# Transposing k by DMA instead of on TensorE, from the seventh step on, in a fused retention and MLP kernel

## The chip, the cores and the metric

The kernel runs on one core of one Trainium2 chip. The metric is the device time of one execution in microseconds (us), lower is better. Most executions of a kernel agree within about 1%; those that came out over 1.5% above the fastest of their kernel are marked slow and named below. A version is called faster or slower when the ratio of its times to those of the kernel before is clear of 2%.

The engines are called as in the profile: PE (TensorE matmuls), PEld (its weight loads), DVE (VectorE), ACT (ScalarE), POOL (GpSimd), SP (SyncE). SP computes nothing; it issues DMAs, one after the other, and waits where an issue needs somebody else's result.

## The reference

```python
# attention part: B = 8, H = 8 heads, S = 576, D = 64, all float32
scores = q @ k.transpose(0, 1, 3, 2) / sqrt(D)
ret    = scores * Dmat                    # Dmat = gamma_h ** (i - j) for i >= j, else 0
x      = (ret @ v)                        # -> (4608 tokens, 512)
# MLP part
h    = x @ w_in                           # 512 -> 1024
solu = h * softmax(h)
ln   = (solu - mean) / sqrt(var + 1e-6) * g_ln
out  = ln @ w_out                         # 1024 -> 512
```

## The kernel before

The work is cut into 36 steps of the attention part (`i`: 256 tokens, four heads) and 36 tiles of 128 tokens of the MLP part (`t`). Every small piece of work is an operation with a name: `ldk5` loads k of step 5, `sk5` scales it to float16 on POOL, `T5` transposes q and k of step 5 on PE, `qe5` copies the result from PSUM to SBUF on ACT, `S5` makes the scores, `M1_5` and `M2_5` are the two GEMMs of tile 5, `out5` stores it. Each engine works through a fixed list of these names. The first half of each list (`FIRST`) is written out, the rest follows from sort keys. A small list model with a duration for each kind of operation (`DUR`) only decides the program order; the chip decides the time.

```python
DUR = dict(T=0.45, ..., qe=1.0, ..., ld=0.89, ldw=1.34, out=0.72, lm=0.42)
CAP = dict(raw=5, qk16=3, v16=4, tp=1, qkT=3, s=1, ...)        # buffers of each kind

def load(i, nm, src):                       # 128 x 512 float32, issued by SP
    ...
    if wi < 2:
        nc.sync.dma_start(out=t, in_=...)                       # one issue, 256 KB
    else:
        for r in range(4):                                      # four issues of 64 KB
            nc.sync.dma_start(out=t[32 * r : 32 * r + 32], in_=...)

def qk_tp(i):                               # T: eight 128x128 transposes on PE
    tp = pools["tp"].tile([P, 2, 2, 2, P], F16, ...)
    for n, src in enumerate((d["q16"], d["k16"])):
        for hp in range(2):
            for j in range(2):
                nc.tensor.transpose(out=tp[:, n, hp, j],
                                    in_=src[:, j, 2 * hp : 2 * hp + 2, :], identity=ident)

def qk_ev(i):                               # qe: 1024 columns, PSUM to SBUF, on ACT
    nc.scalar.copy(out=d["qkT"], in_=d["tp"])

def x_ev(i):                                # xe: attention output, input of the first GEMM
    nc.scalar.copy(out=d["xT"].rearrange("p c h q -> p c (h q)"), in_=d["av"][:, :, 0:256])

def store(t):                               # out: even and odd rows apart, two issues a tile
    for j in range(2):
        q_dma = nc.scalar if t == NT - 1 and j else nc.sync
        if wi < 2:
            q_dma.dma_start(out=out[r0 : r0 + P, :].rearrange("(q j) m -> j q m", j=2)[j],
                            in_=tk[t]["osb"][64 * j : 64 * j + 64])
        ...                                 # wi == 2: two pieces each, four issues a tile

op(f"T{i}",  "PE",  "T",  [f"sq{i}", f"sk{i}"], ...)
op(f"qe{i}", "ACT", "qe", [f"T{i}"], ...)
op(f"S{i}",  "PE",  "S",  [f"qe{i}"], ...)
```

The softmax here doesn't subtract the row's maximum and nothing guards it: scores larger than these inputs give would overflow.

Of the kernel before, what the change touches and what calls it, by code (L numbers as in the profile page):

```python
# [10 lines left out]
F16 = mybir.dt.float16  # L11
P = 128
# [1 line left out]

DUR = dict(
    T=0.45, L=0.45, M1=1.73, M2=1.73, I=0.23, S=0.23, V=0.23, K=0.14, G=0.1,
    qe=1.0, xe=0.59, ex=1.22, le=1.0, oe=0.69, wi=0.6, wg=0.66, cva=0.6,
    mask=1.22, st_a=0.29, so=1.22, bn=1.68, od=0.7, wib=0.55, wgd=0.5, WM=1.73, nw=0.62, wf=0.66, wp=1.04, sqd=0.7, gc=0.2,
    sq=1.03, sk=1.03, st_b=0.4, cast=0.84, rs=0.6, cv=0.61,
    ld=0.89, ldw=1.34, out=0.72, lm=0.42,  # L20
)
PE_OUT = 0.2
PER = 5.36
START = dict(SP=2.3)
WARM = 31.0
NE = 14

FIRST = dict(
    ACT=(
        "cv0 qe0 cv1 qe1 xe0 wi1a wi2a wi0a xe1 wi3a ex0 qe2 wg0 le0 wg2 qe3 wg4 wg6 ex1 xe2 "  # L30
        "nw1 nw0 xe3 qe4 wf1 ex2 qe5 wf3 le1 xe4 qe6 wf2 ex3 le2 xe5 oe0 qe7 wf0 ex4 le3 xe6 "
        "qe8 ex5 le4 xe7 qe9 oe1 ex6 le5 oe2 qe10 xe8 ex7 le6 xe9 qe11 oe3 ex8 le7 oe4 wf6 "
        "qe12 xe10 wf4 ex9 le8 xe11 oe5 wf7 qe13 ex10 le9 xe12 wf5 qe14 oe6 ex11 le10 xe13 "
        "oe7 qe15 oe8 ex12 le11 xe14 qe16 oe9 ex13 le12 xe15 qe17 oe10 ex14 le13"
    ),
    DVE=(
        "gc sq0 sa0 sd0 sq1 mask0 wi1b sa1 sd1 mask1 wi2b wi0b wi3b sa2 sd2 so0 mask2 wg1 sa3 "
        "sd3 wg3 wg5 wg7 mask3 so1 bn0 sa4 sd4 bn1 mask4 so2 od0 sa5 sd5 mask5 bn2 sa6 sd6 "
        "so3 mask6 od1 bn3 sa7 sd7 so4 mask7 od2 bn4 sa8 sd8 so5 mask8 bn5 sa9 sd9 so6 od3 "
        "mask9 bn6 so7 od4 sa10 sd10 mask10 bn7 so8 od5 sa11 sd11 mask11 bn8 sa12 so9 sd12 "  # L40
        "od6 mask12 bn9 sa13 sd13 so10 od7 mask13 bn10 so11 sa14 sd14 od8 bn11 mask14 so12 "
        "sa15 sd15 od9 mask15 bn12 so13 od10 mask16 bn13 so14"
    ),
    PE=(
        "G K0 T0 S0 T1 I0 V0 K1 S1 I1 V1 M1_0 T2 K2 S2 L0 I2 V2 K3 T3 M1_1 S3 WM I3 V3 K4 T4 "
        "M1_2 S4 T5 M2_0 L1 I4 V4 K5 S5 T6 M1_3 I5 V5 K6 S6 L2 M2_1 T7 M1_4 I6 V6 K7 S7 L3 "
        "M2_2 T8 M1_5 I7 V7 K8 S8 L4 M2_3 T9 M1_6 I8 V8 K9 L5 S9 T10 M1_7 L6 I9 M2_4 V9 K10 "
        "S10 T11 M1_8 L7 I10 M2_5 V10 K11 S11 T12 M1_9 L8 I11 V11 K12 S12 M2_6 T13 M1_10 I12 "
        "V12 K13 S13 L9 M2_7 T14 M1_11 I13 L10 M2_8 V13 K14 S14 T15 M1_12 L11 M2_9 I14 V14 "
        "K15 S15 T16 M1_13 L12 I15 S16 V15 M2_10 T17 M1_14 L13 I16 S17 V16 M2_11"  # L50
    ),
    POOL=(
        "sk0 sk1 sm0 sc0 sm1 sc1 sq2 sk2 cv2 sk3 sm2 sc2 cv3 sq3 sm3 sc3 sk4 sq4 cv4 sq5 sk5 "
        "sm4 sc4 sq6 rs0 cv5 sk6 sq7 sm5 sc5 cv6 cv7 sk7 sm6 sk9 sc6 sk8 sq8 wp0 rs1 sm7 sc7 "
        "cv8 sq9 cv10 cv9 wp3 sm8 sk10 sc8 cv12 wp2 sq10 sq11 sq12 sm9 sc9 sk11 cv11 sk12 wp1 "
        "sm10 sc10 sk13 rs2 sq13 sq14 cv14 sm11 sc11 sk14 rs3 wp6 sm12 sc12 cv13 sq16 cv15 "
        "cv16 sm13 sc13 wp4 sk15 sq15 sk16 wp5 rs4 sm14 sc14 sq17 wp7 sk17 rs5 cv17 sm15 sc15 "
        "sq18 sk18 cv18 sq19 sk19 cv19"
    ),
    SP=(  # L60
        "ldk0 ldv0 ldq0 ldk1 ldq1 lm ldv1 lwi1 lwi2 lwi0 lwi3 ldq2 ldk2 ldv2 ldk3 lwo0 ldv3 "
        "ldq3 lwo2 lwo4 lwo6 ldk4 ldq4 ldv4 ldq5 ldk5 ldq6 ldv5 ldk6 ldv7 ldq7 ldq9 ldk7 ldk8 "
        "ldv6 ldq10 ldv8 ldk9 ldq11 ldq8 ldv10 ldk10 ldv11 ldq14 ldk11 ldk14 ldv9 ldv12 ldq12 "
        "ldk12 ldk13 ldq16 out0 out1 ldk17 ldv16 ldq15 ldq13 ldv13 out2 ldv14 ldq17 ldk16 "
        "out4 ldv15 ldk15 out3 out5 out7 out6 ldv17 ldv18 ldq19 ldk18 ldv19 ldq18 ldk19 ldq20 "
        "out8 ldk20 ldv20 out9 ldq21 ldk21 ldv21"
    ),
)
HOP = 0.06
# [104 lines left out]
def kernel(  # L174
# [10 lines left out]
    nc = tc.nc  # L185
    B, H, S, D = q.shape
    NTOK, DM = out.shape
    DFF = moe_w_in.shape[1]
    ACT = mybir.ActivationFunctionType
# [2 lines left out]
    small_np, masks_np, id_np = _np_tables()  # L192


    CAP = dict(raw=5, qk16=3, v16=4, tp=1, qkT=3, s=1, ret=2, xy=1, gw=6, s160=4, s161=9, tt=2,
               xT=5, h=1, e=2, oc=2, solu=3, sml=8, lnT=4, o=1, osb=3)
    pools = {}
    PS = bass.MemoryType.PSUM
# [36 lines left out]
    st = [dict() for _ in range(NS)]  # L235
    tk = [dict() for _ in range(NT)]
# [43 lines left out]
    def cast_v(i, copy):  # L280
        t = pools["v16"].tile([P, 4, 2, D], F16, tag="v16", name="v16")
        copy(out=t, in_=st[i]["vr"])
        st[i]["v16"] = t

    def qk_tp(i):
        d = st[i]
        tp = pools["tp"].tile([P, 2, 2, 2, P], F16, tag="tp", name="tqk")
        for n, src in enumerate((d["q16"], d["k16"])):
            for hp in range(2):
                for j in range(2):  # L290
                    nc.tensor.transpose(  # L291
                        out=tp[:, n, hp, j], in_=src[:, j, 2 * hp : 2 * hp + 2, :], identity=ident
                    )
        d["tp"] = tp

    def qk_ev(i):
        d = st[i]
        d["qkT"] = pools["qkT"].tile([P, 2, 2, 2, P], F16, tag="qkT", name="qkT")
        nc.scalar.copy(out=d["qkT"], in_=d["tp"])  # L299


    ee = [slice(0, 64), slice(64, 128)]
# [34 lines left out]
    def scores(i):  # L337
        d = st[i]
        s_ps = pools["s"].tile([P, 2, 2, 2, P], FP, tag="s", name="s_ps")
        sv = s_ps.rearrange("p e h j (a q) -> p e h j a q", a=2)  # L340
        qkT = d["qkT"]
        for hp in range(2):
            for j in range(2):
                for c in range(2):
                    for e in range(2):
                        nc.tensor.matmul(  # L346
                            out=sv[ee[c], e, hp, j], lhsT=qkT[ee[e], 1, hp, j, ee[c]],
                            rhs=qkT[ee[e], 0, hp, :, ee[c]], start=True, stop=True,
                        )
        d["s"] = s_ps  # L350
# [142 lines left out]
    def mm2(t):  # L493
# [6 lines left out]
        for c in range(8):  # L500
            nc.tensor.matmul(  # L501
                out=d["o"], lhsT=d["lnT"][:, c], rhs=(w2g16 if t < NE else w2c16)[:, c], start=(c == 0), stop=(c == 7)
            )
# [10 lines left out]
    def o_ev(t):  # L514
        d = tk[t]
        d["osb"] = pools["osb"].tile([P, DM], FP, tag="osb", name="o_sb")
        nc.scalar.activation(  # L517
            out=d["osb"], in_=d["oc"] if t < NE else d["o"], func=ACT.Copy,
            scale=ws[t // 2]["rs"][:, t % 2 : t % 2 + 1],
# [59 lines left out]
    def op(name, eng, kind, deps, key, emit, bufs=()):  # L579
        key = rank.get(name, PER * key[0] + key[1])  # L580
        ops.append(Op(name, eng, DUR[kind], [x for x in deps if x], key, emit, bufs))

    for i in range(NS):
        w, hf = divmod(i, 2)
        b, wi = wins[w]
        full = wi < 2
# [4 lines left out]
        op(f"sq{i}", "DVE" if early else "POOL", "sqd" if early else "sq", [f"ldq{i}"], (i - 2, 1.8),  # L591
           lambda i=i, e=nc.vector if early else nc.gpsimd: scale(i, "q", 0, e), [("q16", [f"T{i}"])])
        op(f"sk{i}", "POOL", "sk", [f"ldk{i}"], (i - 2, 2.9), lambda i=i: scale(i, "k", 32, nc.gpsimd),
           [("k16", [f"T{i}", f"K{i}" if full else ""])])
        op(f"cv{i}", "ACT" if early else "POOL", "cva" if early else "cv", [f"ldv{i}"], (i - 1, 0.0),
           lambda i=i, c=nc.scalar.copy if early else nc.gpsimd.tensor_copy: cast_v(i, c),
           [("v16", [f"V{i}", f"K{i}" if full else ""])])
        op(f"T{i}", "PE", "T", [f"sq{i}", f"sk{i}"], (i - 1, 2.73), lambda i=i: qk_tp(i), [("tp", [f"qe{i}"])])
        op(f"qe{i}", "ACT", "qe", [f"T{i}"], (i - 1, 3.6), lambda i=i: qk_ev(i), [("qkT", [f"V{i}"])])
        op(f"S{i}", "PE", "S", [f"qe{i}"], (i, 0.3), lambda i=i: scores(i), [("s", [f"mask{i}"])])  # L600
        op(f"mask{i}", "DVE", "mask", [f"S{i}", "lm"], (i, 3.2), lambda i=i: mask(i), [("ret", [f"V{i}"])])
        if full:
            op(f"K{i}", "PE", "K", [f"sk{i}", f"cv{i}"] + [f"V{i - 1}" if i else ""], (i, 0.8), lambda i=i: kv_mm(i))
# [15 lines left out]
    for t in range(NT):  # L619
        w, c = divmod(t, 2)  # L620
# [6 lines left out]
        if c:  # L627
            op(f"rs{w}", "POOL", "rs", [f"bn{t - 1}", f"bn{t}"], (m + 2, 0.77), lambda w=w: rstd(w), [("sml", [f"oe{t}"])])
        op(f"L{t}", "PE", "L", [f"so{t}"], (m + 1, 4.9), lambda t=t: ln_tp(t), [("tp", [f"le{t}"])])
        op(f"le{t}", "ACT", "le", [f"L{t}"], (m + 2, 0.97), lambda t=t: ln_ev(t), [("lnT", [f"M2_{t}"])])  # L630
        o_end = f"od{t}" if t < NE else f"oe{t}"
        op(f"M2_{t}", "PE", "M2", [f"le{t}"] + [f"{'wg' if t < NE else 'wp'}{x}" for x in range(8)], (m + 4, 1.0),
           lambda t=t: mm2(t), [("s" if late(t) else "o", [o_end])])
        if t < NE:
            op(o_end, "DVE", "od", [f"M2_{t}", "nw0"], (m + 4, 2.9), lambda t=t: o_mean(t), [("oc", [f"oe{t}"])])
# [4 lines left out]
    for c in range(4):  # L640
# [4 lines left out]
        out=masks, in_=nc.inline_tensor(masks_np, name="masks").ap().rearrange("p (m j) -> p m j", m=2)))  # L645
    op("G", "PE", "G", ["ldk0"], (0, 0.0), g_tp, [("h", ["gc"])])
    op("gc", "DVE", "gc", ["G"], (0, 1.0), lambda: nc.vector.tensor_copy(out=gln, in_=cur["g_ps"][:, 0:8]))
    for c in range(0, 8, 2):
        op(f"lwo{c}", "SP", "ldw", [], (-2 + c / 8, 0.6), lambda c=c: nc.sync.dma_start(out=w2_f[:, c : c + 2], in_=w2_v[:, c : c + 2]))
        for x in (c, c + 1):  # L650
            op(f"wf{x}", "ACT", "wf", ["gc", "nw1"], (8 + x * 0.75, 1.9), lambda x=x: nc.scalar.activation(
                out=w2_f[:, x], in_=w2_f[:, x], func=ACT.Copy, scale=gln[:, x : x + 1]))
# [5 lines left out]
    for x in range(2):  # L658
        op(f"nw{x}", "ACT", "nw", ["WM"], (5, 1.1), lambda x=x: nc.scalar.activation(
            out=nws[:, x], in_=cur["w_sum"], func=ACT.Copy, scale=1.0 if x == 0 else 1.0 / DFF))  # L660
# [7 lines left out]
    with tc.manual_schedule():  # L668
# [14 lines left out]
        for o in sorted(ops, key=lambda o: start[o.name]):  # L683
            if o.eng == "PE":
                fill = fill and o.name[:2] != "M2"
                if fill and 6.0 < start[o.name] < WARM:
                    for _ in range(int((start[o.name] - end_pe - 0.3) / 0.36)):
# [33 lines left out]
```

## Time and profile before

| | before |
|---|---|
| median, first three runs | 226.03 us (225.61 to 1063.31; the 1063 is one outlier that stays unexplained) |
| PE busy, whole run | 207.0 us of 224.9 (92%) |
| PE busy from 105 to 207 us | 101.86 us of 102 |
| SP in issue entries, 40 to 180 us | 94 of 140 us (67%) |
| POOL waiting for loads, whole run | 13.0 us |

Lines of the page of the kernel before. First busy time and instructions by engine, then busy tenths in 40 slices of the run (with the clock that PE was granted and the mean share of the 16 DMA engines), the main DMA queue with the share of the engines' time that its packets took, the chain of work that ended last, and one group of instructions (busy us, mean ns of one | idle before it):

```profile
span 224.9 us, 7378 instructions
PE 207.0 (92%) x2985; PEld 121.8 (54%) x2985; DVE 181.5 (81%) x320; ACT 163.2 (73%) x238; POOL 151.8 (67%) x231
...
PE   7776989899699999699999999999999999999991
...
PEclk9999999999999999999999999999999999999998
DMA  6999999995576610799988776777763552222324
...
q1 hardware_dynamic: 65200, 41.96, 66.9%
...
PE 63%; DVE 17%; DMA 9%; POOL 4%; issue 2%; SPq 2%; ACT 1%; DVEq 0%; POOLq 0%; ACTq 0%
...
L299 ACT COPY qkT<-tqk 128x1024 f16<-128x1024 f16 x36 | 36.3, 1008 | 9.3 <-PE tqk L291 9.1
```

The second half of the run is PE alone. The chain of waits shows one step of it (start, us, what): second GEMM, transposes of q and k, first GEMM.

```profile
146.42 1.83 PE o_ps L501 x8
148.25 0.45 PE tqk L291 x8
148.70 1.73 PE h_ps L431 x8
```

The windows view of the same kernel (stretch, its length, then busy us of PE, PEld, DVE, ACT, POOL, the clock, the DMA share, GB/s):

```profile
60.00:80.00 20.00, 19.12 (x314) 11.43 (x314) 18.87 (x32) 16.47 (x25) 18.55 (x29) 1.00 0.66 182
...
105.00:207.00 102.00, 101.86 (x1529) 62.26 (x1528) 86.65 (x153) 77.66 (x114) 68.67 (x108) 1.00 0.62 167
```

The timeline of SP's queue (start, us, what). The page has a load of 256 KB landing (all its data in place) 4.6 to 4.8 us after its issue:

```profile
107.29 0.51 SPq L259 DMA_DIRECT2D kr<-in_k_dram  x1
107.89 0.50 SPq L259 DMA_DIRECT2D vr<-in_v_dram  x1
108.48 1.12 SPq L529 DMA_DIRECT2D out_dram<-o_sb  x2
```

The sums are taken record by record from the trace; the timeline merges neighbours of one kind and shows the gaps between them as part of the entry. Some entries are much longer than others of their kind (a load can take over 2 us); they count in full.

### The profile page before, as it was taken

To read this page: it belongs to the slowest core of one execution; us is meant where nothing else is said; L and a number is where in the kernel's file an instruction comes from. 1 tells how busy PE (TensorE), PEld (TensorE's weight loads), DVE (VectorE), ACT (ScalarE), POOL (GpSimd) and SP (SyncE) were. 2 spreads that over 40 slices of the span, in tenths; PEclk is the share of its full clock that TensorE was granted. 3 is DMA by queue.
4 is the path that set the end of the run, shared out by engine and by line. 5 is a ranking of instruction groups with operands and counts; after the bars stand their busy time and mean duration, and the time that the engine had idled before them with its cause. 6 is when DMAs were issued, how large, how long until landed. Compare 5 with 4: busy or idle time off the path is not lost.

```text
span 224.9 us, 7378 instructions
## 1 busy us (share of the span) xinstructions
PE 207.0 (92%) x2985; PEld 121.8 (54%) x2985; DVE 181.5 (81%) x320; ACT 163.2 (73%) x238; POOL 151.8 (67%) x231
## 2 busy tenths in 40 slices
PE   7776989899699999699999999999999999999991
PEld 2433445556455556465666666665666666555440
DVE  6654788999999998999999888888887888876540
ACT  3555889776869988578787777777777777776751
POOL 3429599899989989829578869695968677311010
PEclk9999999999999999999999999999999999999998
DMA  6999999995576610799988776777763552222324
GB/s 176 360 344 348 320 262 287 286 279 157 128 224 173 195 24 13 188 305 293 267 235 247 215 195 192 214 191 191 218 184 109 153 131 52 50 47 60 84 69 119
DMA packets 65635, 42.64 MB, mean 190 GB/s; under 512 B 4024, under 2 KB 59456, under 8 KB 65600
## 3 DMA queue, kind: packets, MB, share of 16 engines
q1 hardware_dynamic: 65200, 41.96, 66.9%
q8 instruction: 23, 0.38, 0.8%
q10 hardware_dynamic: 400, 0.21, 0.5%
q14 instruction: 12, 0.10, 0.2%
HBM read 32.71 MB, written 9.44 MB: 187 GB/s over the span
## 4 chain that ended last, share of the span: by engine, by line
PE 63%; DVE 17%; DMA 9%; POOL 4%; issue 2%; SPq 2%; ACT 1%; DVEq 0%; POOLq 0%; ACTq 0%
PE h_ps L431 21%; PE o_ps L501 21%; PE xy L311 6%; PE tln L480 5%; PE tqk L291 4%; DMA qr<-in_q_dram 4%; DVE solu L451 4%; PE s_ps L346 4%; DVE bs L457 3%; DVE ret L379 3%; DMA vr<-in_v_dram 3%; DMA kr<-in_k_dram 2%; DVE oc L509 2%; SPq L259 2%; DVE w L465 1%
## 5 line engine op out<-in xcount | busy, mean ns | idle before, releaser
L431 PE MATMUL h_ps<-w_in_122,xT 128*128 128x512 f16 x288 | 68.0, 379 | 2.0 <-DVE solu L451 1.9
L451 DVE TENSOR_TENSOR solu<-h_ps,e_sb 128x1024 f16<-128x1024 f32 x36 | 43.9, 1219 | 13.4 <-ACT e_sb L444 13.2
L444 ACT ACTIVATE e_sb<-h_ps 128x1024 f32<-128x1024 f32 x36 | 36.8, 1022 | 18.2 <-PE h_ps L431 17.9
L457 DVE BATCH_NORM_STATS2 bs<-solu 128x6 f32<-128x512 f16 x72 | 46.0, 680 | 0.1
L379 DVE TENSOR_TENSOR ret<-s_ps,masks 128x1024 f16<-128x1024 f32 x36 | 43.7, 1215 | 0.6 <-PE s_ps L346 0.4
L299 ACT COPY qkT<-tqk 128x1024 f16<-128x1024 f16 x36 | 36.3, 1008 | 9.3 <-PE tqk L291 9.1
L431 PEld LDWEIGHTS <-xT 128*128 128x128 f16 x288 | 27.0, 98 | 29.1 <-issue 2.8
L501 PEld LDWEIGHTS <-lnT 128*128 128x128 f16 x288 | 25.9, 98 | 27.2
L488 ACT COPY lnT<-tln 128x1024 f16<-128x1024 f16 x36 | 36.2, 1005 | 3.5 <-PE tln L480 3.5
L501 PE MATMUL o_ps<-w2c_124,lnT 128*128 128x512 f16 x160 | 38.0, 380 | 0.0
L501 PE MATMUL o_ps<-w2g_123,lnT 128*128 128x512 f16 x112 | 26.5, 380 | 0.0
L419 ACT CAST xT<-xy 128x512 f16<-128x512 f32 x36 | 21.4, 594 | 6.6 <-PE xy L311 6.2
L404 POOL TENSOR_TENSOR g<-tt,small 128x128 f32<-128x128 f32 x32 | 13.4, 418 | 15.3 <-DVE tt L400 15.3
L480 PEld LDWEIGHTS <-solu 128*128 128x128 f16 x288 | 18.5, 98 | 8.7 <-DVE solu L451 1.7
L517 ACT ACTIVATE o_sb<-o_ps,rs 128x512 f32<-128x512 f32 x20 | 13.7, 687 | 12.7 <-PE o_ps L501 6.9
L480 PE MATMUL tln<-ident,solu 128*128 128x128 f16 x288 | 22.0, 219 | 0.9 <-DVE solu L451 0.9
L346 PE MATMUL s_ps<-qkT 64*64 64x128 f16 x576 | 14.9, 220 | 0.8 <-ACT qkT L299 0.7
L346 PEld LDWEIGHTS <-qkT 64*64 64x64 f16 x576 | 9.5, 107 | 4.6 <-ACT qkT L299 1.8
L395 DVE TENSOR_TENSOR g<-xy,g 128x128 f32<-128x128 f32 x16 | 4.6, 289 | 8.7 <-PE xy L311 5.2
L400 DVE TENSOR_TENSOR tt<-xy,g 128x128 f32<-128x128 f32 x32 | 9.3, 292 | 2.7 <-ACT xT L419 0.7
L509 DVE SCALAR_TENSOR_TENSOR oc<-nws,mv,o_ps 128x512 f32<-128x512 f32 x14 | 10.3, 738 | 0.2 <-PE o_ps L501 0.2
L517 ACT ACTIVATE o_sb<-oc,rs 128x512 f32<-128x512 f32 x14 | 10.2, 728 | 0.3 <-DMA qr<-in_q_dram 0.3
(507 smaller groups left out, 336.9 us busy)
## 6 DMA issues: line engine op xcount, KB each, us to landing
kr<-in_k_dram SPq DMA_DIRECT2D x32, 256.0 KB, 4.6
vr<-in_v_dram SPq DMA_DIRECT2D x32, 256.0 KB, 4.8
qr<-in_q_dram SPq DMA_DIRECT2D x32, 256.0 KB, 4.8
out_dram<-o_sb SPq DMA_DIRECT2D x64, 128.0 KB, 2.4
w_in_f<-in_moe_w_in_dram SPq DMA_DIRECT2D x4, 512.0 KB, 5.9
w_f<-in_moe_w_out_dram SPq DMA_DIRECT2D x4, 512.0 KB, 8.0
qr<-in_q_dram SPq DMA_DIRECT2D x16, 64.0 KB, 2.3
kr<-in_k_dram SPq DMA_DIRECT2D x16, 64.0 KB, 2.0
```

What stands on the lines that cost most here:

```text
L299: nc.scalar.copy(out=d["qkT"], in_=d["tp"])
L346: nc.tensor.matmul(out=sv[ee[c], e, hp, j], lhsT=qkT[ee[e], 1, hp, j, ee[c]], rhs=qkT[ee[e], 0, hp, :, ee[c]], start=True, stop=True,)
L379: nc.vector.tensor_tensor(out=d["ret"].rearrange("p e h j q -> p (e h) (j q)"), in0=d["s"].rearrange("p e h j q -> p (e h) (j q)"), in1=ma ...
L419: nc.scalar.copy(out=d["xT"].rearrange("p c h q -> p c (h q)"), in_=d["av"][:, :, 0:256])
L431: nc.tensor.matmul(out=h_ps[:, hh], lhsT=st[2 * w + dc // 2]["xT"][:, c, dc % 2], rhs=w_in16[:, dc, hh], start=(dc == 0), stop=(dc == 3),)
L444: nc.scalar.activation(out=d["e"], in_=d["h"], func=ACT.Exp, accum_out=ws[w]["se"][:, c : c + 1])
L451: nc.vector.tensor_tensor(out=d["solu"], in0=d["h"], in1=d["e"], op=ALU.mult)
L457: nc.vector.bn_stats(out=bs[:, half], in_=tk[t]["solu"][:, half * 512 : half * 512 + 512])
L480: nc.tensor.transpose(out=tp[:, c], in_=d["solu"][:, c * P : (c + 1) * P], identity=ident)
L488: nc.scalar.copy(out=d["lnT"], in_=d["tp"])
L501: nc.tensor.matmul(out=d["o"], lhsT=d["lnT"][:, c], rhs=(w2g16 if t < NE else w2c16)[:, c], start=(c == 0), stop=(c == 7))
L517: nc.scalar.activation(out=d["osb"], in_=d["oc"] if t < NE else d["o"], func=ACT.Copy, scale=ws[t // 2]["rs"][:, t % 2 : t % 2 + 1],)
```

## The change

The intent: PE is full, and four of its eight transposes in each step are those of k. From the seventh step on a transposing DMA makes them, from SBUF to SBUF (called "the crossbar" below). PE then has 0.22 us less to do in each of 30 steps, and ACT copies 512 columns instead of 1024. Loads get a sixth buffer, and the lists of all engines are written out for the whole run, ordered with the model for the new program. The diff is shortened: `...` stands for what is cut, and a few one-line changes that follow from those shown are left out.

```diff
-PER = 5.36
+PER = 5.14
+ND = 6
 DUR = dict(
-    qe=1.0, ...
+    T2=0.23, qe=1.0, qe2=0.59, tk=1.05, ...
 FIRST = dict(...)      # all five lists are new, to the end of the run (cut here)
-    CAP = dict(raw=5, qk16=3, v16=4, tp=1, qkT=3, ...
+    CAP = dict(raw=6, qk16=3, v16=4, tp=1, qkT=3, kT=3, ...
+    def k_tp(i):
+        d["kT"] = pools["kT"].tile([P, 2, 2, P], F16, tag="kT", name="kT")
+        nc.sync.dma_start_transpose(
+            out=d["kT"].rearrange("p j h t -> p (j h) t"),
+            in_=d["k16"].rearrange("p j h d -> p (j h d)"),
+        )
-        for n, src in enumerate((d["q16"], d["k16"])):
+        for n, src in enumerate((d["q16"], d["k16"]) if i < ND else (d["q16"],)):
-        nc.scalar.copy(out=d["qkT"], in_=d["tp"])
+        nc.scalar.copy(out=d["qkT"][:, :n], in_=d["tp"][:, :n])
+        dma_k = i >= ND
+        if dma_k:
+            op(f"tk{i}", "SP", "tk", [f"sk{i}"], ..., lambda i=i: k_tp(i), [("kT", [f"S{i}"])])
-        op(f"T{i}", "PE", "T", [f"sq{i}", f"sk{i}"], ...)
+        op(f"T{i}", "PE", "T2" if dma_k else "T", [f"sq{i}"] + ([] if dma_k else [f"sk{i}"]), ...)
-        op(f"S{i}", "PE", "S", [f"qe{i}"], ...)
+        op(f"S{i}", "PE", "S", [f"qe{i}"] + ([f"tk{i}"] if dma_k else []), ...)
```

## The prediction

> **What bounds it now.** Three stretches. (1) Until about 40 us the kernel fills: the windows view gives the DMA engines a share of 0.99 and 1.04 in the first two 20 us stretches, and the chain of waits runs over loads and POOL. (2) From 40 to 104 us DVE is busy 19.2, 18.9 and 18.4 us of each 20 and PE 18.2, 19.1 and 18.0; the chain alternates between DVE and PE, and ten steps (q/k transposes at 48.85 to 105.26 us) take 5.64 us each. (3) From 105 to 207 us PE is busy 100% and the chain is PE alone, about 5.3 us a step: two GEMMs of 1.73 to 1.83, transposes of the normalised tile 0.45, q/k transposes 0.45, scores and state work about 0.9.
>
> **What the change does.** In 30 of 36 steps the four k transposes leave PE. In the timeline the k group starts 0.22 to 0.24 us after the q group, so they cost PE 0.22 us a step, 6.7 us in all. The ACT copy of the transposed q/k (1.01 us for 1024 columns) halves; a 512-column copy (xT, groups view) took 0.59, so ACT loses about 0.4 us a step, 12 us in all, off the chain in stretch 3. DVE and POOL do the same work. SP gets 30 transposing DMAs of 128 KB, SBUF to SBUF, each waiting for POOL's scaled k; scores now wait for that DMA as well. A sixth load buffer lets loads start earlier. The instruction order beyond step 17 is now a fixed list.
>
> **On the critical path.** Stretch 3: the chain holds 17 q/k groups from 111 to 196 us, so 17 x 0.22 = 3.7 us. Stretch 2: DVE work per step is unchanged, so the 0.22 us there is mostly hidden; but at 5.64 us a step there are stalls (POOL waits 4.0 us for a late q load at 101 us; DMA moves only 24 and 13 GB/s about 79 to 90 us), which the new order, the sixth buffer and lighter ACT can partly recover: 1 to 3 us. Tail: nothing. Expected gain about 5.5 us.
>
> **The risk is the DMA.** No trace here has a transposing DMA. The Trainium skill, "VectorE: DVE Perf Modes" (The three transpose paths), gives 1309 ns for one 128x128 block through the crossbar; "Advanced Engine Details and Errata" (X-Bar Transpose) says such DMAs are about as fast as ordinary ones. Ordinary 256 KB loads took 4.6 to 4.8 us to land, so I estimate 2 to 5 us here, queued behind loads. K is scaled well over 5 us before its scores (for example 101.2 to 103.2 scaled, scores of that step after 108), barely enough. If the transposes take several times that of engine time, the loads behind them, at a DMA share of 0.74 to 0.93 in 100 to 140 us, come late and stretch 3 gets holes. SP works in order, so a transpose waiting for POOL also holds back loads.
>
> **Predicted: 220.5 us** (80%: 216 to 228). Faster by over 2%: 0.55; within 2%: 0.30; slower by over 2%: 0.15.
>
> **What would show it.** Right: q transposes alone take 0.22 us; the copy to qkT about 0.59 us; PE still 99 to 100% busy after 105 us with about 5.05 us a step; PE busy total near 200 us; scores hardly wait for the kT DMA; ACT busy near 151 us. Stretch 2 down to about 5.4 us a step.
> Wrong: scores waiting for kT on the chain; DMA share at 1 after 100 us and POOL waiting for loads; SP's wait list headed by POOL's k; kT landing later than 5 us; PE below 97% in stretch 3; or DVE taking over as the bound there (it had 16.2 to 17.2 of 20 us).

## The result, and the profile after

The changed kernel takes 240.1 us (median; 238.98 to 240.56 in four runs) against 226.23 us: a ratio of 1.0615 with a 95% interval of 1.0564 to 1.0667. It is slower by 6%. Ratios here and below are the mean time of one kernel's fast runs over that of the other's of the same rounds, so not quite the ratio of the medians that are quoted.

The lines of the page of the changed kernel that answer to those above. PE is as busy in microseconds, but holes have come into the second half, the clock dips after them, and the chain that was PE for 63% now runs over DMA, POOL and SP's queue:

```profile
span 238.4 us, 7123 instructions
PE 206.8 (87%) x2862; PEld 116.8 (49%) x2862; DVE 177.6 (75%) x320; ACT 151.4 (64%) x238; POOL 151.7 (64%) x231
...
PE   7876899997949986999999798999872799999992
...
PEclk9999999999997999799999999999999599999999
DMA  7999997999589688799997897696877254323073
...
q1 hardware_dynamic: 81520, 45.89, 79.3%
...
PE 39%; DMA 20%; POOL 15%; SPq 14%; ACT 4%; issue 4%; DVE 3%; POOLq 0%; ACTq 0%; DVEq 0%
```

What was to be saved was saved. The groups view, shapes apart, has the copy at 583 ns where it had 1008, and PE's trace has 123 matmuls fewer (30 x 4 = 120 were taken out; a few records can be missing):

```profile
L344 ACT COPY qkT<-tqk 128x512 f16<-128x512 f16 x30 | 17.5, 583 | 9.0 <-PE tqk L335 9.0
```

The windows view shows where it went: PE lost 10.7 of the 102 us of its full stretch.

```profile
60.00:80.00 20.00, 16.90 (x238) 9.66 (x237) 13.65 (x25) 12.97 (x22) 13.41 (x20) 0.91 0.80 192
...
105.00:207.00 102.00, 91.31 (x1345) 53.05 (x1344) 79.57 (x140) 65.00 (x105) 72.34 (x111) 0.97 0.82 184
```

PE's list of waits (us in total, times, longest) is headed by scores that waited for a transposed k:

```profile
PE s_ps L392 <- DMA kT<-k_3927: 5.6, 1, 5.6
PE s_ps L392 <- DMA kT<-k_1415: 3.1, 1, 3.1
...
PE s_ps L392 <- DMA kT<-k_1110: 1.2, 1, 1.2
```

The longest of them can be followed. POOL's timeline has this k scaled by 175.5 us:

```profile
174.46 1.04 POOL L310 TENSOR_TENSOR k_3927<-kr,small 128x512 f16<-128x512 f32 x1
```

SP's timeline shows why its transpose began only at 182.7. It stood in the list behind another step's transpose, the stores of two tiles, a four-part load and one more load, over 7 us of issuing without a pause:

```profile
175.40 2.12 SPq L324 DMA_TRANSPOSE kT<-k_3864  x1
177.62 2.45 SPq L575 DMA_DIRECT2D out_dram<-o_sb  x4
180.12 2.02 SPq L302 DMA_DIRECT2D kr<-in_k_dram  x4
182.19 0.43 SPq L295 DMA_DIRECT2D vr<-in_v_dram  x1
182.72 1.23 SPq L324 DMA_TRANSPOSE kT<-k_3927  x1
```

PE's timeline has the hole of 5.65 us before the scores, and then a second GEMM that lasts 3.59 us in this view where the chain of the kernel before has 1.83; the windows view shows the granted clock at half speed for these four microseconds:

```profile
186.05 0.64 PE L392 MATMUL s_ps<-qkT,kT 64*64 64x128 f16 x16 [5.65 <-DMA kT<-k_3927]
...
187.45 3.59 PE L547 MATMUL o_ps<-w2c_127,lnT 128*128 128x512 f16 x8
```

The windows view over the same microseconds, in two stretches of four:

```profile
182.00:186.00 4.00, 0.00 (x0) 0.00 (x0) 1.23 (x1) 0.83 (x2) 0.56 (x2) 0.76 0.58 144
186.00:190.00 4.00, 3.95 (x30) 2.12 (x31) 3.19 (x6) 1.50 (x2) 3.75 (x7) 0.50 0.16 33
```

The Trainium skill, page "TensorE: Matmul & The Clock Gate" (Why this matters for your kernels), warns of idle gaps of more than about 3 us between matmuls, after which PE falls back to half its clock. This trace agrees in kind: a 5.65 us gap, then 0.50. As a limit the 3 us are not sharp here: the same trace grants half the clock for 3.4 us after a gap of 2.54 us (PE idle from 93.1, half clock from 95.3) and the full clock after one of 2.31 us (from 172.1), and in run e10 below a gap of 3.19 us (from 130.0) passed without a drop. So a late input can cost PE more than its own wait.

SP's issue entries now fill 124 of the 140 us from 40 to 180 (94 before), and POOL waits 25 us for loads (13 before). Over the whole run the 30 transposes hold SP for 39.9 us; all its other entries take 143.9 us, where they took 144.4 before. So the transposes came on top, and nothing made room for them.

### The profile page after: what moved, and what is told of

It reads as the page before. It is cut to its first block, busy times and chain, and to the rows that moved or that the text cites. A ratio compares the mean times of both kernels' runs of the same rounds, so it can differ in the third digit from the quotient of the medians.

```text
span 238.4 us, 7123 instructions
## 1 busy us (share of the span) xinstructions
PE 206.8 (87%) x2862; PEld 116.8 (49%) x2862; DVE 177.6 (75%) x320; ACT 151.4 (64%) x238; POOL 151.7 (64%) x231
## 3 DMA queue, kind: packets, MB, share of 16 engines
q1 hardware_dynamic: 81520, 45.89, 79.3%
## 4 chain that ended last, share of the span: by engine, by line
PE 39%; DMA 20%; POOL 15%; SPq 14%; ACT 4%; issue 4%; DVE 3%; POOLq 0%; ACTq 0%; DVEq 0%
PE o_ps L547 14%; PE h_ps L477 10%; DMA kr<-in_k_dram 6%; DMA qr<-in_q_dram 6%; SPq L295 5%; SPq L302 5%; PE xy L356 4%; PE tln L526 4%; SPq L575 3%; DMA out_dram<-o_sb 3%; PE s_ps L392 2%; POOL w2c_127 L618 2%; PE tqk L335 2%; DMA masks<-masks 2%; DVE solu L497 2%
## 5 line engine op out<-in xcount | busy, mean ns | idle before, releaser
L534 ACT COPY lnT<-tln 128x1024 f16<-128x1024 f16 x36 | 36.5, 1013 | 16.0 <-PE tln L526 15.8
L547 PEld LDWEIGHTS <-lnT 128*128 128x128 f16 x288 | 27.1, 100 | 28.8 <-issue 3.7
L547 PE MATMUL o_ps<-w2c_127,lnT 128*128 128x512 f16 x160 | 39.5, 392 | 0.0
L344 ACT COPY qkT<-tqk 128x512 f16<-128x512 f16 (+1 forms) x36 | 23.6, 654 | 13.7 <-PE tqk L335 13.7
L547 PE MATMUL o_ps<-w2g_126,lnT 128*128 128x512 f16 x112 | 28.4, 399 | 0.0
L526 PE MATMUL tln<-ident,solu 128*128 128x128 f16 x288 | 23.0, 225 | 1.1 <-ACT qkT L344 0.7
L392 PE MATMUL s_ps<-qkT,kT 64*64 64x128 f16 x480 | 12.5, 224 | 10.0 <-DMA kT<-k_3927 5.6
L439 DVE COPY g<-xy 128x128 f32<-128x128 f32 x16 | 4.5, 281 | 12.9 <-PE xy L356 11.0
L392 PEld LDWEIGHTS <-kT 64*64 64x64 f16 x480 | 8.4, 111 | 11.3 <-DMA kT<-k_3927 5.8
```

The source lines that it names most:

```text
L344: nc.scalar.copy(out=d["qkT"][:, :n], in_=d["tp"][:, :n])
L392: nc.tensor.matmul(out=sv[ee[c], e, hp, j], lhsT=kT[ee[e], hp, j, ee[c]], rhs=qkT[ee[e], 0, hp, :, ee[c]], start=True, stop=True,)
L526: nc.tensor.transpose(out=tp[:, c], in_=d["solu"][:, c * P : (c + 1) * P], identity=ident)
L534: nc.scalar.copy(out=d["lnT"], in_=d["tp"])
L547: nc.tensor.matmul(out=d["o"], lhsT=d["lnT"][:, c], rhs=(w2g16 if t < NE else w2c16)[:, c], start=(c == 0), stop=(c == 7))
```

## The experiments

Four theories were to be told apart.

- **S**: SP's single in-order queue is short of issue time. Each transpose takes it 1.2 us, all 30 of them 39.9 us.
- **D**: the crossbar transposes take time on the 16 DMA engines, and the loads behind them come late.
- **L/W**: the dependencies. The scores wait for a landing that takes microseconds (L), or SP stands waiting for POOL's scaled k and holds back loads (W).
- **O**: the new order or the sixth buffer is bad by itself.

The columns of this table: the median; the ratio to the kernel before of the same rounds, with its interval; SP's issue entries from 40 to 180 us; the time that the packets of the SP and ACT queues took on the 16 DMA engines (their shares added, times the span); and POOL's waits for loads. The last three come from the one profiled execution.

| run | median us | ratio (95%) | SP us of 140 | DMA engines us | POOL waits us |
|---|---|---|---|---|---|
| before | 226.2 | 1 | 94 | 152 | 13 |
| changed | 240.1 | 1.062 (1.056 to 1.067) | 124 | 190 | 25 |
| e1 new order, k on PE | 224.9 | 0.991 (0.985 to 0.996) | 94 | 155 | 9 |
| e2 old order, crossbar | 244.2 | 1.075 (1.070 to 1.079) | 116 | 191 | 18 |
| e3 half of the stores from ACT | 234.9 | 1.032 (1.028 to 1.037) | 109 | 186 | 14 |
| e4 plain copy for the crossbar | 233.2 | 1.026 (1.020 to 1.032) | 116 | 169 | 21 |
| e5 crossbar issued from ACT | 235.4 | 1.040 (1.033 to 1.047) | 93 | 197 | 12 |
| e6 = e1 + unused crossbar | 237.6 | 1.050 (1.042 to 1.059) | 126 | 193 | 28 |
| e7 = e6, waits for nobody | 237.8 | 1.051 (1.043 to 1.059) | 121 | 199 | 25 |
| e8 = e7 with plain copies | 229.0 | 1.012 (1.004 to 1.020) | 116 | 174 | 15 |
| e9 = e1 + tiny copies | 232.4 | 1.026 (1.020 to 1.033) | 123 | 157 | 21 |
| e10 = e1 + large copies | 240.6 | 1.065 (1.057 to 1.073) | 125 | 206 | 26 |
| e11 crossbar in the last 8 steps | 229.5 | 1.015 (1.009 to 1.022) | 96 | 165 | 14 |
| e12 changed, 1/8 of the output bytes | 238.6 | 1.056 (1.048 to 1.064) | 125 | 157 | 21 |
| g1 changed, searched order | 232.8 | 1.022 (1.014 to 1.031) | 117 | 185 | 19 |
| g2 e1, searched order | 232.2 | 1.023 (1.016 to 1.030) | 88 | 153 | 8 |
| g3 changed, 1/16 of the output bytes, half the stores | 226.5 | 0.995 (0.985 to 1.004) | 114 | 160 | 13 |
| g5 changed, one store a tile | 228.8 | 1.005 (0.995 to 1.014) | 111 | 186 | 13 |
| g6 e1, one store a tile | 225.5 | 0.993 (0.986 to 1.000) | 76 | 145 | 8 |
| g7 changed, two transposes moved forward | 238.1 | 1.050 (1.044 to 1.057) | 125 | 185 | 29 |

The medians are of all four runs of a kernel, slow ones too. Marked slow were one run each of e3, g1, g3 and g7 and two of e12; the fast runs alone have means of 234.6 (e3), 232.2 (g1), 225.9 (g3), 237.5 (g7) and 236.7 (e12: 235.91 and 237.58). The ratio of e12 counts its two slow runs (239.59 and 240.41). The profiled runs of e3, g1 and g7 were slow ones; their three last columns are given for completeness and nothing below rests on them alone. Those of e6, e7 and e10 were the slowest of their four, by about 1%. The rounds ran on different chips, with medians of the kernel before between 225.8 and 227.5, so a difference of 1 us between runs of different rounds says nothing.

### e1: the new order, k transposed on PE as before

```diff
-ND = 6
+ND = 36
 SP=( ... )     # the names tk6 to tk35 taken out of SP's list
```

> The changed kernel's instruction order and sixth load buffer, but every k still transposed by TensorE (the 30 crossbar DMAs gone). Theory S (SP's one in-order issue queue is overfilled by the 30 transposes at 1.2 us each) and theory D (the crossbar transposes take 1.3 us of all 16 DMA engines each): 222 to 229 us, near before. Rival O (the fixed order for the whole run is bad by itself): 234 us or more, most of the loss stays.

Measured: 224.87 us. The order and the sixth buffer are not the loss (O falls); they are worth about 1%. Against the kernel before the gain is small: the interval lies below 1, but within the 2% that count as same.

### e2: the order of before, k by crossbar

```diff
 # FIRST, PER and raw=5 of the kernel before; tk6 ... tk19 put into SP's list
 # behind the place where the list model has sk done; the rest by key
```

> The kernel before with its own order and five load buffers, k from the seventh step on by crossbar; each transpose is put into SP's list behind the model's end of its scaling. S and D: slower than before, 230 us or more. O: 226 us or less, as the transposes alone would then be harmless or a gain.

Measured: 244.17 us. The crossbar alone costs 18 us in the old order and 15 in the new (changed against e1). The new order was a better place for it, not a worse one.

### e3: half of the stores from ACT's queue

```diff
-            q_dma = nc.scalar if t == NT - 1 and j else nc.sync
+            q_dma = nc.scalar if j else nc.sync
```

> The changed kernel, but the second half of each output tile is stored from ACT's queue: SP loses about 36 x 0.6 = 22 us of issue time and some waits, DMA traffic is the same. S: recovers at least 6 us of the 14, 226 to 234 us. D and O: stays at 237 to 242 us.

Measured: 234.88 us (234.6 by the fast runs), between the two forecasts: 5 us came back. The run isn't clean, since ACT is charged what SP saves.

### e4: a plain copy in place of the crossbar transpose

```diff
-        nc.sync.dma_start_transpose(out=..., in_=...)
+        kp = pools["kT"].tile([P, 2, 2, P + 16], F16, tag="kT", name="kT")
+        d["kT"] = kp[:, :, :, 0:P]
+        nc.sync.dma_start(out=kp.rearrange("p j h t -> p (j h) t")[:, :, 0:P], in_=...)
```

> The changed kernel with each crossbar transpose replaced by a plain SBUF to SBUF copy of the same 128 KB in 256-byte pieces (result wrong on purpose). Issue falls from 1.2 to about 0.5 us, so SP loses about 21 us; DMA engine time per copy is read from the queue's share (the transposes took 1.29 us of 16 engines). S: about the same recovery as storing half of the output from ACT, 226 to 234 us. D: full recovery, below 226, only if the engine time falls well under 1.29 us, and no recovery if it does not. O: 237 or more.

Measured: 233.22 us with a wrong result. Both costs fall with a plain copy (issue 0.65 us, engines (169.3 - 154.9) / 30 = 0.5 us each, against 1.2 and (190.0 - 154.9) / 30 = 1.2 us), and 7 us come back. So the run separates nothing, but it shows that the crossbar is dearer than a copy of the same bytes in both.

### e5: the crossbar transposes from ACT's queue

```diff
-        nc.sync.dma_start_transpose(
+        nc.scalar.dma_start_transpose(
-            op(f"tk{i}", "SP", "tk", ...)
+            op(f"tk{i}", "ACT", "tk", ...)     # and the names moved into ACT's list
```

> The changed kernel, the 30 crossbar transposes issued from ACT's queue instead of SP's, so SP's list is that of the order-only run (224.9 us) and nothing on SP waits for POOL's scaled k. ACT gains 30 x 1.2 = 37 us of issue time (about 4.2 + 1.2 = 5.4 us a step) and their waits. Theory S (SP's queue: issue time and hold-ups): recovers to 225 to 233 us, and POOL hardly waits for loads. Theory D (time on the DMA engines): 236 us or more, POOL still waits for loads. If ACT becomes the bound: 235 or more with ACT over 90% busy plus issuing, and PE waiting for ACT's copies.

Measured: 235.4 us, between the forecasts of S and D. POOL's waits fell to 12 us, as S says, so loads are on time again when SP is free of the transposes. But PE now waits for ACT's copies (3.5 + 1.8 + 1.8 us) and 5.1 us for kT. ACT is a poor place: it needs 1.21 us for each issue too, 150.9 us of work and 38 us of issues in 233 us (the 90% of the forecast was not reached). The Trainium skill, "DMA: Bandwidth & Descriptors" (Issuing engines are not separate DMA queues), says that issuing from several engines saves only sequencer time; here that time is what is short, and moving it moves the shortage.

### e6 and e7: the cost of the crossbar without its use

Both add to e1 the 30 transposes at the changed kernel's places in SP's list, and nobody reads the result. In e6 they read POOL's scaled k and wait for it. In e7 they read a constant tile and wait for nobody.

```diff
 # e6: k is transposed on PE as in e1, kT is written and never read
-[("kT", [f"S{i}"])]
+[("kT", [f"tk{i}"])]
-        kT = d["kT"].rearrange("p j h t -> p h j t") if i >= ND else qkT[:, 1]
+        kT = qkT[:, 1]
 # (cut: T, qe and the copy as in e1; k16 is held until tk has read it)
 # e7 besides (cut: tk depends on the load of the masks instead of on sk, and k16 is not held):
-            in_=d["k16"].rearrange("p j h d -> p (j h d)"),
+            in_=masks.rearrange("p m j -> p (m j)"),
```

> The order-only kernel plus the 30 crossbar transposes on SP exactly where the change has them, with their wait for POOL's scaled k, but nobody reads their result: TensorE transposes k as before. Against the order-only run (224.9) it shows the cost of issue, DMA time and SP's waits, without the latency of the scores' dependency. S and D: 232 us or more. L (the loss is the scores waiting for the landing of kT): 227 us or less.

> As the dummy run above, but the crossbar transposes read a constant tile, so SP waits for nobody before them. The difference to that run is W, SP's in-order waiting for POOL. If W is most: 228 us or less here and 232 or more there. If issue and engine time are most: both about the same, 232 or more.

Measured: 237.59 and 237.81 us. This is the first clear answer. Most of the loss is there (about 13 us above e1) when nobody waits for the transposes and they wait for nobody: L and W fall as main causes. What remains is what a crossbar transpose takes by being issued and carried out. It shows as late loads: POOL waits 28 and 25 us for them, against 9 in e1. The changed kernel is another 2.5 us above e6, which is not clear of noise (their intervals overlap), although PE has 6.7 us less to do in it (30 x 0.22). So what was saved on PE did not show in the time. The scores' waits for kT (9.9 us in its profile) may have eaten it; this was not taken apart further.

### e8, e9 and e10: issue time and engine time apart

The view by line has the issues of e7's transposes on SP's queue (count: minimum, median and maximum in ns, first and last start):

```profile
L324 SPq DMA_TRANSPOSE kT<-masks x30: 1200/1282/3579, 36.9 to 197.8; - x30
```

In e8, e9 and e10 these dummies are replaced by plain transfers. e8: one copy of 128 KB in 256-byte pieces. e9: two copies of 4 KB. e10: one copy of 352 KB in 256-byte pieces.

```diff
 # e9
+        for n in range(2):
+            nc.sync.dma_start(out=kp[:, n], in_=masks[:, n, 0:16])
 # e10
+        nc.sync.dma_start(out=kp[:, :, 0:64],
+                          in_=w_in_f[:, 0, 0:704].rearrange("p (n t) -> p n t", t=64))
```

> As the run above, but a plain copy of the constant tile in 256-byte pieces: issue 0.65 instead of 1.22 us, 0.5 instead of 1.3 us of the 16 DMA engines each. Between the order-only run (224.9) and the free crossbar dummy, in proportion to the cost: about 40 to 50% of that run's loss. If only a crossbar transpose hurts (it holds up other transfers beyond its own time), 226 us or less.

> The order-only kernel with each dummy crossbar transpose replaced by two tiny copies of 4 KB (32 bytes a partition) from the constant tile: about 1.1 us of SP issue time as the transpose has, hardly any time on the DMA engines. S (issue time): 233 us or more, like the free crossbar dummy (237.8). D (engine time): 227 us or less, like the order-only run (224.9).

> The order-only kernel with each dummy crossbar transpose replaced by one plain copy of 352 KB in 256-byte pieces: the issue of one copy (about 0.65 us, as in the plain-copy dummy that gave 229.0) and about 1.3 us of the 16 DMA engines, as the transpose. D: 235 us or more. S: 230 us or less, as the plain copy of 128 KB.

The view by tile has the same for the added transfers. For the tiny copies of e9:

```profile
L325 SPq DMA_DIRECT2D kT<-masks x60: 466/599/1725, 35.1 to 190.9; - x60
```

For the large copies of e10:

```profile
L324 SPq DMA_DIRECT2D kT<-w_in_f x30: 605/656/2274, 34.5 to 199.7; - x30
```

The main DMA queue of e1, from its page, is the base for the engine times below:

```profile
q1 hardware_dynamic: 65200, 41.96, 68.8%
```

With the small share of ACT's queue (0.5%) that is 69.3% of 223.5 us, 155 us. The engine time of one added transfer is what a run has above this, over 30.

| added to e1, 30 times | issue us each | engines us each | time against e1 |
|---|---|---|---|
| e9, two tiny copies | 2 x 0.60 | 0.1 | +7.5 us |
| e8, one plain copy | 0.65 | 0.6 | +4.2 us |
| e10, one large copy | 0.66 | 1.7 | +15.8 us |
| e7, one crossbar transpose | 1.3 | 1.5 | +12.9 us |

e9 came out at 232.4, just under the forecast of S; e10 inside that of D; e8 at a third of the loss of e7 where 40 to 50% were expected. Neither S nor D has the loss to itself. The issue time of the transposes, with hardly any bytes, costs 7.5 us; engine time alone can cost even more when there is enough of it. The two can't be kept quite apart: in e10 SP's other entries, the same loads and stores as in e1, took 168.6 us in all where they took 142.9 in e1 and 142.5 in e9, so e10 fills SP's queue as much as e9 does (125 and 123 us of 140). In e7 these other entries took 141.5 us, as in e1: there the engine time of the transposes did not lengthen them. The times against e1 are across rounds; taken by the ratios they are larger by under 1.5 us, in the same order.

### e11: only the last eight steps by crossbar

```diff
-ND = 6
+ND = 28
```

> A candidate: the changed kernel's order and buffers, but only the last eight steps take k by crossbar, where the order-only run's DMA share is 0.25 to 0.5 from 160 us on. S and D alike: no harm, a gain of up to 8 x 0.22 = 1.8 us over the order-only run, 222.5 to 225 us. If a single late landing already costs more than it saves: 226 or more.

Measured: 229.45 us, slower than e1 by 4.6 (against the kernel before the verdict is unclear). The candidate fails. Its one wait of scores for kT is 5.5 us long; the transposes stand in SP's list where the changed kernel has them, behind stores and four-part loads.

### e12 and g3: engine time away, then both away

```diff
 # e12: 64 of 512 columns are stored
-                    in_=tk[t]["osb"][64 * j : 64 * j + 64],
+                    in_=tk[t]["osb"][64 * j : 64 * j + 64, 0:64],
 # g3 besides: only every other row
-        for j in range(2):
+        for j in range(1):
```

> The changed kernel, crossbar and all, but only 64 of 512 columns of each output tile are stored (result wrong on purpose): the same DMA issues and waits, about 30 us less time on the DMA engines. D: recovers at least 7 of the 14 us, 233 us or less. S: 237 us or more.

> The changed kernel with one 64-column store of half the rows for each output tile (result wrong on purpose): about 22 us less issue time and about 33 us less engine time, together what the 30 transposes cost. S and D together: 229 us or less. If something else about the crossbar makes the loss (latency of its landing, POOL's hold-up): 233 us or more.

Measured: 238.59 and 226.54 us, both with a wrong result. By its median e12 lies where S had it; its two fast runs (mean 236.7) lie just below that, and above D's 233. Of the main queue's share of the engines, e12 has this left (79.3% of 238.4 us in the changed kernel):

```profile
span 234.1 us, 7122 instructions
...
q1 hardware_dynamic: 81520, 37.75, 66.8%
```

Taking 33 us off the DMA engines (190 to 157) without touching the issues gives back 1.5 us by the medians and 3.4 by the fast runs. Taking away half of the stores' issues as well gives back 11 to 12 us more. In the changed kernel the engines are secondary; SP's queue is what binds.

### g5 and g6: one store instead of two, correct

The two stores of a tile are there because even and odd tokens lie in different halves of the partitions. If ACT puts the tokens in natural order when it copies the attention output (a write with a stride of two elements), each tile is one store of 256 KB (the few tiles that had four stores have two). The bytes are the same.

```diff
-        nc.scalar.copy(out=d["xT"].rearrange("p c h q -> p c (h q)"), in_=d["av"][:, :, 0:256])
+        nc.scalar.copy(
+            out=d["xT"].rearrange("p c h (q j) -> p (c h) j q", j=2),
+            in_=d["av"][:, :, 0:256].rearrange("p c (h j q) -> p c h j q", h=2, j=2))
-        for j in range(2): ...two stores
+        nc.sync.dma_start(out=out[r0 : r0 + P, :], in_=tk[t]["osb"])
```

> The changed kernel with token order made natural when ACT copies xT (strided write), so that each output tile needs one store of 256 KB instead of two of 128 KB: about 36 x 0.6 = 21 us less SP issue time, the same bytes, results correct. S as the larger share: 232 us or less. D as the larger share: 235 us or more. A cost of the strided copy would show in the xT copy's mean (0.59 us).

> Control and candidate: the same single store in the order-only kernel, which still transposes k on TensorE (224.9 us). SP was not full there, so 222 to 226 us; if the crossbar is to be of use, the run above must beat this one.

Measured: 228.78 and 225.52 us, both correct. In the changed kernel the stores' issue entries fall from 43.4 to 20.7 us, the engines keep 186 of their 190 us of work, and 11 of the 14 us come back, although ACT pays for it: the groups view of g5 has the strided copy at 738 ns, which was 588:

```profile
L465 ACT CAST xT<-xy 128x512 f16<-128x512 f32 x36 | 26.6, 738 | 8.0 <-DVE tt L446 2.6 <-PE xy L356 2.2 <-DVE g L441 1.5
```

The larger stores hold SP no longer each than the smaller ones did, in the view by line (changed kernel, then g5):

```profile
L575 SPq DMA_DIRECT2D out_dram<-o_sb x64: 466/587/1652, 45.5 to 230.7; - x64
L574 SPq DMA_DIRECT2D out_dram<-o_sb x32: 332/448/1423, 45.9 to 219.5; - x32
```

This is S shown in the changed kernel itself. The number of transfers falls with their issue time, so a limit on the number alone would look the same; no run separates the two. POOL's waits for loads are back at 13 us. On e1, where SP has room, the same edit brings nothing (225.5 against 224.9). And even with it, the crossbar version doesn't beat the one that transposes k on PE.

### g1 and g2: another order, searched with measured durations

The list model that ordered the changed kernel has 1.05 us for a transpose, 0.72 for the stores of a tile and 0.89 for a load even where that is four issues; on the chip these are 1.2, 1.1 and 2.0. All five lists were searched anew with the measured durations and with two assumptions of the model, a cap on the transfers in flight and one shared engine time, once with the crossbar (g1) and once with k on PE (g2).

```diff
 FIRST = dict(...)      # all five lists replaced, nothing else
```

> The changed kernel, only the five fixed lists are new: searched with a list model in which SP's issues and landings have the durations of these traces (transpose 1.24, load 0.55 or 4 x 0.48, store 2 x 0.58 or 4 x 0.46 us[...], one shared DMA engine time). If the order made for cheaper transfers is the cause: 220 to 228 us. If the load itself is (no order hides it): 233 us or more.

> Control: the same search on the order-only kernel (k by TensorE throughout). If the search itself brings something it is seen here: 222 to 227 us expected, against 224.9. The crossbar is worth having only if the run above beats this one.

Measured: 232.8 and 232.2 us. The control failed: the search made e1 slower by 7 us, so this search is worse than the one that made the lists. That it made the crossbar kernel faster by 7 us and brought the two level shows that the price of the crossbar depends on the order. It doesn't show how low it can get. This stays open.

### g7: the two late transposes moved forward

```diff
-"tk31 out21 out22 ldk35 ldv31 tk30 tk32"
+"tk31 tk30 out21 out22 ldk35 ldv31 tk32"
-"ldq16 out2 ldq12 out1 ldv13 tk11"
+"ldq16 tk11 out2 ldq12 out1 ldv13"
```

> The changed kernel with two entries of SP's list moved forward: the transposes of step 11 (before two stores and two loads) and of step 30 (before two tiles' stores, a four-part load and a load). If the two late landings (8.7 us of waiting, and about 3 us of lowered clock after them) are the loss: 228 to 234 us. If SP is short of issue time everywhere, the holes move to other waits (POOL for loads): 236 to 241 us.

Measured: 238.06 us (237.5 by the fast runs). This is in the range of the second forecast: 2 to 2.5 us were gained. In the profile, which is of the slow run (240.6 us), so only the shift of kind is read from it, PE's waits for kT fell from 9.9 to 2.5 us, and the list has new heads:

```profile
PE tqk L350 <- POOL q L325: 6.6, 3, 5.0
PE xy L371 <- POOL sbd L474: 6.3, 8, 2.4
...
PE s_ps L407 <- DMA kT<-k: 2.5, 4, 0.9
```

What was moved forward pushed stores and loads back. The wait for kT was where the shortage showed, not where it came from.

## Why the prediction was wrong

**Right, and measured so.** PE was the bound after 105 us. Four transposes less a step, the ACT copy at 0.59 us (583 ns), ACT busy near 151 us (151.4): all as written. The landing of kT, estimated at 2 to 5 us, was 2.4 to 5.8 with a middle of 3.3. Of its own signs for being wrong, three came true: scores waited for kT (9.9 us in all, three times), POOL waited for loads (25 us), and PE was at 89.5% in stretch 3.

**The step that failed: "SP gets 30 transposing DMAs".** They were counted but not costed. The trace of before showed 0.5 us of SP's time for a load and 1.1 for a tile's stores, and summing them would have shown a queue filled to 67% in the middle of the run. The transposes took 1.2 us each, 39.9 us of entries in all, and filled it to 89%. Taking out 23 us of other issues (g5) gives 11 of 14 us back; adding 38 us of issue time alone to e1 (e9) costs 7.5.

**"The risk is the DMA" looked at the wrong part of it.** The text feared engine time and landing time. Engine time is real: a crossbar transpose took 1.2 to 1.5 us of all 16 engines, 2.3 to 2.4 times a plain copy of the same bytes, where the prediction leaned on "about as fast as ordinary ones". But less engine time alone gave back only 1.5 to 3.4 us (e12), and e6 and e7 have most of the loss with nobody waiting for the landing; what the landing cost besides was not measured by itself. "Loads come late and stretch 3 gets holes" did come true (POOL's waits 13 to 25 us), by SP's queue more than by the engines (e12 and g5).

**"A transpose waiting for POOL also holds back loads"** was not the cause: with and without that wait the dummies took 237.6 and 237.8 us.

**"The new order, the sixth buffer and lighter ACT can partly recover: 1 to 3 us."** The order and buffer alone brought 0.9% (e1), about 2 us. That part of the gain was real, and was never the crossbar's.

**PE busy total "near 200 us" was 206.8,** with fewer matmuls. Three holes of PE (3.1, 2.5 and 5.7 us) went with 13.6 us at half clock, in which PE was busy for 11.3. At full clock that work would have taken about half, 5.7 us less (an estimate), which is most of the 6.7 us that was saved.

**The chances.** Slower by over 2% got 0.15. With a queue at 67% and, as it turned out, 39.9 us of new entries it deserved more.

## What to carry to other kernels

Count the issuing queue as an engine: sum the entries of its timeline before adding transfers to it, and cost each new transfer twice, by its issue and by its time on the DMA engines. Here an offload that freed the fullest engine by 0.22 us a step was no gain, because it took 1.2 us of an in-order queue that feeds the same engine and had no room for it. And when moving one late transfer forward only makes another one late, look for the resource that is short, not for the place.

## What the Trainium skill lacked or had wrong

- "Advanced Engine Details and Errata" (X-Bar Transpose) says that transposing DMAs are as fast as regular ones, at about 90% of a copy. Here 128 KB from SBUF to SBUF took 1.2 us (changed kernel) to 1.5 us (e7) of the 16 engines; a plain copy of the same bytes in 256-byte pieces took 0.5 (e4) to 0.6 us (e8).
- "DMA: Bandwidth & Descriptors" (DMA Transpose (X-bar)) gives no issue time; the only such counts on the page stand in its part on trn3. Here a 128x512 transpose held the issuing queue for 1.2 us, on SP and on ACT alike, against 0.5 us for a plain load and 0.65 for the copy.
- The same page (Issuing engines are not separate DMA queues) calls the issue time usually small relative to the DMA itself. Here a transpose's issue (1.2 us) was as long as its time on the 16 engines (1.2 us in the changed kernel), and e9 lost 7.5 us to 60 copies of 4 KB that took hardly any engine time.
- "VectorE: DVE Perf Modes" (The three transpose paths) gives 1309 ns for one 128x128 block. No run here has a single block; four blocks in one transfer landed after 2.4 us at best and 3.3 us in the middle.
- "TensorE: Matmul & The Clock Gate" (Why this matters for your kernels) was borne out in kind: 5.65 us of idle, then a granted clock of 0.50. Its figure of about 3 us was no sharp limit: half clock followed 2.54 us of idle (changed kernel), and not 3.19 us (e10).
- No page gives ACT's time for a strided two-byte write ("Advanced Engine Details and Errata", SBUF Cachelines, speaks of strides without times): a 512-column copy went from 588 to 738 ns.
